# Linear attention with a highway layer: the softmax work of batches 2 and 3 and the key/value products moved in the order of issue

## The chip, the cores and the metric

One core of a Trainium2 chip runs the whole program. The metric is the device time of one execution in microseconds (us), the median of several. The kernel before takes 149.44 us (three runs, 148.86 to 149.5); the profiled execution has a span of 146.9 us from its first to its last instruction. The engines are TensorE (PE, with its weight loads PEld), VectorE (DVE), ScalarE (ACT), GpSimd (POOL) and SyncE, whose queue (SPq) issues every DMA. Each works through its own list of instructions in the order in which the program emits them.

## The reference

For each of 8 batches and 8 heads, q, k and v are 576 x 64. A softmax of q over the 64 features and one of k over the 576 positions stand on either side of a small product:

```
q_s = exp(q) / sum(exp(q), over features)
k_s = exp(k) / sum(exp(k), over positions)
kv  = k_s^T v          (64 x 64 per head)
x   = q_s kv           (heads side by side: 4608 rows of 512)
H = relu(x W_h);  T = sigmoid(x W_t + b_t);  out = T*H + (1-T)*x
```

The reference takes maxima off before the exponentials; the kernel does without. Its sigmoid is 0.5 + 0.5 tanh of half the argument.

## The kernel before

Each batch passes through two layers. The **attention part** of batch b consists of these helpers:

- `exp_half` (L150, two halves each for q and k, four heads a half): the exponentials, on ACT.
- `q_sums` (L195, two halves) and `q_recip` (L203), on DVE: the row sums of exp(q) and their reciprocals. Then the scaling of exp(q), for blocks 0 to 3 of its nine row blocks and for 4 to 8: `q_scale_p` (L214) does it on POOL, `q_scale_v` (L206) on DVE, with a small widening cast at L210 and a product at L212.
- `cast_v` (L160, two halves): v to 16 bits, on POOL unless another engine is given.
- `q_trans` (L218, groups of 4, 4 and 1 row blocks): transposes on PE, each followed by a copy from PSUM to `qsT` on DVE (L233).
- `kv_half` (L167, two halves of 36 small products into `psk`): needs half of exp(k) and the same half of the cast v. `kv_norm` (L183, DVE) then divides by the sums of exp(k) and gives `kvn`.
- `x_pair` (L235, two) and `x_left` (L259): the products of `qsT` and `kvn` on PE. Of the four copies of the pairs to `xT`, three are on ACT (L255) and the last on DVE (L257).

The **highway part** of batch c works in four column blocks `ob`: `gate` (four products of 512 columns, then a tanh on ACT, L288), `carry` (four products, then `dd` on DVE, L297) and `blend` (`g` on DVE, L305). `out_tile` turns a finished block back with transposes and copies it out on ACT (L336). The ninth row blocks of all batches (`x9`) form a last highway batch, c = 8.

The order of issue is written out by hand. The head, a list, holds batches 0 and 1 and the highway part of batch 0. From there on the program goes through numbered slots (`at`, L373): slot 8c + 2ob holds `gate(c, ob)`, slot 8c + 2ob + 1 holds `carry(c, ob)`, and slot 8c + 2ob + 2 holds `blend(c, ob)`. Thus eight slots, a stage, do the highway part of batch c and beside it the attention part of batch c + 1. For batch b the stage begins at slot p = 8(b - 1), and "step 3" of it is slot p + 3. Within a slot the functions come in the order in which they were registered, so gate or carry first, then blend, out_tile and the attention work. Whatever follows in the same engine's list waits behind an instruction that isn't ready.

PSUM is shared in rotation: four buffers (`ps_ht`) for gate and carry, so that a gate can start only when the blend two blocks earlier has read its buffer; three (`ps_q`, tag "qx") for `pq`, `psk` and `px`, eleven of which a batch uses in order; one for the output blocks (`nat`). Loads of q, k and v use three buffers each in SBUF, `ek` and `eq` two, `v16` two.

Of the kernel before, what the change touches and what calls it, by code (L numbers as in the profile page):

```python
# [18 lines left out]
def kernel(  # L19
# [10 lines left out]
    nc = tc.nc  # L30
    B, H, S, D = q.shape
    P = 128
    N9 = S // 64
# [339 lines left out]
    def at(p, *fs):  # L373
        events.setdefault(p, []).extend(fs)

    E = lambda f, *a: (lambda: f(*a))

    for c in range(1, B + 1):
        for ob in range(4):
            p = 8 * c + 2 * ob  # L380
# [6 lines left out]
    for g in range(B // 2):  # L387
        p = 16 * (g + 1)
# [5 lines left out]
                at(p + 1 + i // 2, E(out_tile, g, i, True))  # L394
    at(8 * B + 8, E(most9), E(last9))

    for b in range(2, B):
        p = 8 * (b - 1)
        s = p + {2: 0, 3: -4}.get(b, -5)
        at(s, E(exp_half, b, "q", 0))  # L400
        at(s + 1, E(exp_half, b, "q", 1), E(q_sums, b, 0))
        at(s + 2, E(q_sums, b, 1), E(q_recip, b), E(q_scale_p, b, 0, 4))
        if b == 2:
            at(s + 3, E(q_scale_v, b, 4, N9))
        else:
            at(s + 3, E(q_scale_p, b, 4, N9))
        s = p + {2: 2, 3: 0}.get(b, -1)
        at(s, E(exp_half, b, "k", 0))
        at(s + 1, E(exp_half, b, "k", 1))
        s += b == 2  # L410
        at(s, E(cast_v, b, 0))
        at(s + 1, E(cast_v, b, 1))
        tr, kv, x = {
            2: ((4, 4, 5), (5, 6), (7, 7, 7)),
            3: ((2, 3, 4), (4, 5), (6, 6, 7)),
        }.get(b, ((2, 3, 4), (2, 3), (4, 5, 6)))
        for i in range(3):
            at(p + tr[i], E(q_trans, b, i))
        at(p + kv[0], E(kv_half, b, 0))
        at(p + kv[1], E(kv_half, b, 1), E(kv_norm, b))  # L420
        at(p + x[0], E(x_pair, b, 0))
        at(p + x[1], E(x_pair, b, 1))
        at(p + x[2], E(x_left, b))
# [3 lines left out]
    for f in [  # L427
        E(warm_up, 20),
        E(exp_half, 0, "q", 0), E(q_sums, 0, 0),
        E(exp_half, 0, "q", 1), E(q_sums, 0, 1),  # L430
        E(q_recip, 0), E(q_scale_v, 0, 0, 4), E(q_scale_v, 0, 4, N9),
        E(exp_half, 0, "k", 0), E(cast_v, 0, 0),
        E(exp_half, 0, "k", 1), E(cast_v, 0, 1),
        E(q_trans, 0, 0), E(q_trans, 0, 1), E(warm_up, 2), E(q_trans, 0, 2),
        E(warm_up, 6),
        E(kv_half, 0, 0), E(gate_bias), E(warm_up, 2), E(kv_half, 0, 1), E(kv_norm, 0),
        E(warm_up, 4),
        E(x_pair, 0, 0), E(warm_up, 2), E(x_pair, 0, 1), E(warm_up, 2), E(x_left, 0),
        E(warm_up, 14),
        E(exp_half, 1, "q", 0), E(exp_half, 1, "q", 1),  # L440
        E(q_sums, 1, 0),
        *[E(cast_weight, "t", k_, nc.vector) for k_ in range(4)],
        E(q_sums, 1, 1), E(q_recip, 1), E(q_scale_v, 1, 0, 4), E(q_scale_v, 1, 4, N9),
        *[E(cast_weight, "h", k_, (nc.gpsimd, nc.scalar)[k_ % 2]) for k_ in range(4)],
        E(gate, 0, 0), E(gate, 0, 1), E(exp_half, 1, "k", 0), E(cast_v, 1, 0),
        E(carry, 0, 0), E(blend, 0, 0), E(carry, 0, 1), E(blend, 0, 1),
        E(exp_half, 1, "k", 1), E(cast_v, 1, 1),
        E(q_trans, 1, 0), E(q_trans, 1, 1), E(q_trans, 1, 2),
        E(gate, 0, 2), E(carry, 0, 2), E(blend, 0, 2),
        E(kv_half, 1, 0), E(gate, 0, 3), E(kv_half, 1, 1), E(kv_norm, 1),  # L450
        E(carry, 0, 3),
        E(x_pair, 1, 0), E(x_pair, 1, 1), E(blend, 0, 3), E(x_left, 1),
        *[E(load, b, w) for b in (2, 3) for w in "qkv"],
    ]:
        f()
    for p in range(8, 8 * (B + 1) + 1):
# [33 lines left out]
```

## Time and profile before

| engine | busy us (share of the span) |
|---|---|
| PE | 123.6 (84%) |
| DVE | 108.1 (74%) |
| ACT | 87.3 (59%) |
| POOL | 43.2 (29%) |

A stage can be timed by the start of the first product of `gate(c, 0)` in the trace of PE:

| stage (slots) | highway batch, attention batch | starts at us | length us |
|---|---|---|---|
| head | 0, and 0 and 1 | 0 | 34.17 |
| 8 to 15 | 1, 2 | 34.17 | 18.93 |
| 16 to 23 | 2, 3 | 53.10 | 12.39 |
| 24 to 31 | 3, 4 | 65.49 | 11.92 |
| 32 to 39 | 4, 5 | 77.41 | 13.82 |
| 40 to 47 | 5, 6 | 91.23 | 13.82 |
| 48 to 55 | 6, 7 | 105.05 | 13.82 |
| 56 to the end | 7, the ninth blocks, the last outputs | 118.87 | 28.03 |

The shares of the first table are means over stages that have different limits. How the lengths of the second come about is read from the timelines of the engines and from the chain of waits, which runs backwards from the last instruction to what released it.

### The profile page before, as it was taken

The page shows a single profiled execution, that of the slowest core. Times are in us where ns is not written, and L with a number is a line of the kernel's source. Part 1 is how long each engine was busy: PE and PEld are TensorE (multiplying, and loading weights), DVE is VectorE, ACT ScalarE, POOL GpSimd, SP SyncE. Part 2 cuts the span into 40 slices and gives each one's busy share as a digit, 9 for nine tenths or more (in the row PEclk, how much of TensorE's full clock was granted, in tenths as well). Part 3 has the DMA queues.
Part 4 walks back from the last instruction along what each step waited for, and adds up shares of the span by engine and source line. Part 5 has one row for each costly group of instructions (what it writes and reads, how often), then busy time and mean ns, then how long its engine had stood idle before and what let it go on. Part 6 is the DMA issues. An engine that isn't in the chain of part 4 may idle for free.

```text
span 146.9 us, 3530 instructions
## 1 busy us (share of the span) xinstructions
PE 123.6 (84%) x1477; PEld 67.9 (46%) x1477; DVE 108.1 (74%) x201; ACT 87.3 (59%) x126; POOL 43.2 (29%) x37
## 2 busy tenths in 40 slices
PE   4979999688528979979999599959977999999920
PEld 2335345233125336626645364634545455577610
DVE  1493589966997988996899399929983767577750
ACT  3660658336980269798499549936980764465420
POOL 2006011600083069059107900970295000000000
PEclk9999999999975899999999999999999999999996
DMA  4999999999999999403999999630051006047745
GB/s 159 357 402 397 401 400 410 412 414 403 411 408 412 407 411 412 161 0 145 271 407 416 322 411 402 279 149 0 4 228 60 4 0 286 0 176 326 288 178 179
DMA packets 16022, 40.06 MB, mean 273 GB/s; under 512 B 644, under 2 KB 1672, under 8 KB 14984
## 3 DMA queue, kind: packets, MB, share of 16 engines
q1 hardware_dynamic: 16008, 39.85, 70.6%
q8 instruction: 11, 0.18, 0.5%
q14 instruction: 3, 0.02, 0.0%
HBM read 30.41 MB, written 9.44 MB: 271 GB/s over the span
## 4 chain that ended last, share of the span: by engine, by line
PE 45%; DVE 29%; ACT 6%; POOL 6%; issue 4%; DMA 3%; POOLq 3%; SPq 0%; DVEq 0%; ACTq 0%
PE ph L59 14%; PE pt L59 12%; DVE r L199 10%; PE nat L59 6%; DVE dd L297 4%; PE psk L59 4%; POOL eq L216 3%; DVE eq L212 3%; DMA q<-in_q_dram 3%; DVE g L305 3%; POOLq L485 3%; PE pq L64 3%; PE warm L59 3%; PE px L59 3%; DVE qsT L233 2%
## 5 line engine op out<-in xcount | busy, mean ns | idle before, releaser
L288 ACT ACTIVATE pt<-pt,bt 128x512 f32<-128x512 f32 x36 | 24.0, 669 | 36.3 <-PE pt L59 35.9
L216 POOL TENSOR_TENSOR eq<-eq,r 128x1024 f16<-128x1024 f16 (+1 forms) x11 | 22.8, 2096 | 47.2 <-DVE r L204 34.7
L297 DVE SCALAR_TENSOR_TENSOR dd<-ph,xT 128x512 f16<-128x512 f32 x32 | 21.9, 683 | 17.0 <-PE ph L59 17.0
L59 PE MATMUL ph<-xT,w16h 128*128 128x512 f16 x128 | 33.7, 388 | 0.0
L59 PE MATMUL pt<-xT,w16t 128*128 128x512 f16 x128 | 33.2, 383 | 0.0
L305 DVE SCALAR_TENSOR_TENSOR g<-pt,dd 128x512 f16<-128x512 f32 x36 | 24.5, 680 | 1.9
L199 DVE TENSOR_REDUCE r<-eq 128x18 f32<-128x1152 f16 x16 | 21.6, 1347 | 4.4 <-ACT eq L154 4.2
L161 POOL CAST v<-v 128x1152 f16<-128x1152 f32 x16 | 18.6, 1184 | 13.3 <-DMA v<-in_v_dram 13.3
L154 ACT ACTIVATE eq<-q 128x1152 f16<-128x1152 f32 x16 | 18.5, 1173 | 2.6 <-DMA q<-in_q_dram 2.6
L154 ACT ACTIVATE ek<-k 128x1152 f16<-128x1152 f32 x16 | 18.7, 1185 | 2.0 <-DMA k<-in_k_dram 2.0
L59 PEld LDWEIGHTS <-w16t 128*128 128x128 f16 x144 | 12.8, 98 | 14.4 <-issue 1.4
L59 PE MATMUL nat<-half_i,g 128*128 128x128 f16 x140 | 18.7, 219 | 0.0
L59 PEld LDWEIGHTS <-w16h 128*128 128x128 f16 x144 | 12.4, 99 | 12.1 <-issue 1.7
L336 ACT COPY o<-nat 128x512 f32<-128x512 f32 x28 | 16.9, 603 | 1.7 <-issue 1.1
L255 ACT CAST xT<-px 128x512 f16<-128x512 f32 x24 | 13.4, 596 | 7.4 <-PE px L59 7.3
L64 PE MATMUL pq<-ident,eq 128*128 128x128 f16 x144 | 12.8, 231 | 5.7 <-POOL eq L216 4.1
L59 PE MATMUL nat<-ident,xT 128*128 128x128 f16 x128 | 17.3, 219 | 0.0
L59 PE MATMUL warm<-wide,ident 128*128 128x512 f16 x52 | 15.4, 446 | 1.9 <-DVE wide L140 1.9
L59 PEld LDWEIGHTS <-g 128*128 128x128 f16 x144 | 14.1, 98 | 3.8 <-DVE g L305 0.4
L64 PEld LDWEIGHTS <-eq 128*128 128x128 f16 x144 | 9.9, 103 | 9.5 <-POOL eq L216 4.6
L59 PEld LDWEIGHTS <-xT 128*128 128x128 f16 x128 | 12.5, 98 | 3.3
L59 PE MATMUL psk<-v,ek 64*64 64x65 f16 x576 | 8.1, 197 | 6.8 <-POOL v L161 5.5
(42 smaller groups left out, 91.6 us busy)
## 6 DMA issues: line engine op xcount, KB each, us to landing
out_dram<-o SPq DMA_DIRECT2D x8, 1024.0 KB, 4.3
q<-in_q_dram SPq DMA_DIRECT2D x7, 1152.0 KB, 13.6
k<-in_k_dram SPq DMA_DIRECT2D x7, 1152.0 KB, 14.6
v<-in_v_dram SPq DMA_DIRECT2D x6, 1152.0 KB, 14.6
v<-in_v_dram SPq DMA_DIRECT2D x4, 576.0 KB, 10.7
q<-in_q_dram SPq DMA_DIRECT2D x2, 576.0 KB, 4.0
k<-in_k_dram SPq DMA_DIRECT2D x2, 576.0 KB, 6.9
w32t<-in_moe_w_t_dram SPq DMA_DIRECT2D x1, 1024.0 KB, 12.9
```

Of the source, the lines that this page charges most:

```text
L59: mm = lambda o, l, r, st, sp: nc.tensor.matmul(o, l, r, start=st, stop=sp, skip_group_check=True)
L64: nc.tensor.matmul(o, i, ident, is_transpose=True, start=True, stop=True, skip_group_check=True,)
L154: nc.scalar.activation(dst[b][:, :, 2 * a : 2 * a + 2, :], in32[which][b][:, 2 * a : 2 * a + 2].rearrange("p c n d -> p n c d"), AF.Exp,)
L161: (eng or nc.gpsimd).tensor_copy(v16s[b % 2][:, :, 2 * a : 2 * a + 2, 0:64], in32["v"][b][:, 2 * a : 2 * a + 2].rearrange("p c n d -> p n ...
L199: nc.vector.reduce_sum(qsum[b][:, :, h], eq[b][:, :, h, :], axis=AX.X)
L212: nc.vector.tensor_mul(e, e, r2.unsqueeze(2).broadcast_to([P, w, 32, 2]))
L216: nc.gpsimd.tensor_mul(e, e, r.broadcast_to(list(e.shape)))
L255: nc.scalar.copy(dst, t[c])
L288: nc.scalar.activation(ps, ps, AF.Tanh, bias=bt2[:, ob : ob + 1], scale=0.5)
L297: nc.vector.scalar_tensor_tensor(dd, ps, 0.0, xv(ob), op0=ALU.max, op1=ALU.subtract)
L305: nc.vector.scalar_tensor_tensor(gv(ob), th, 1.0, dd, op0=ALU.add, op1=ALU.mult)
L336: nc.scalar.copy(o, flat(t))
```

## The change

It alters only the order of issue and which engine does two pieces of batch 2. Arithmetic, tiles and buffers stay.

- **Batch 2**: its exponentials of q go up into the head, between the products of batch 1, with the first half of the sums; the second half of the sums and the reciprocal stand first in slot 8. The second scaling is on POOL (`q_scale_p`) instead of DVE. The first half of v is cast on POOL ahead of the scaling, the second on DVE in slot 11. The key/value products come at steps 3 and 4, ahead of most transposes (4, 5, 5); the pairs come at steps 6 and 7.
- **Batch 3**: its exponentials of q move from slots 12 and 13 to 14 and 15, those of k stay in 16 and 17, both casts of v come before both scalings on POOL, and the transposes and products take the steps that batch 2 has.
- **Batch 4** gets what batch 3 had: exponentials of q at slots 20 and 21, of k at 24 and 25, products of k and v at steps 4 and 5, pairs at step 6.
- **Batches 5 to 7**: key/value products at steps 3 and 4 instead of 2 and 3, pairs and rest at 5, 6 and 7 instead of 4, 5 and 6.

The loads of batches 2 and 3 stand earlier in the text; the DMA queue holds the same order.

```diff
+    at(8, E(q_sums, 2, 1), E(q_recip, 2), E(cast_v, 2, 0), E(q_scale_p, 2, 0, 4))
+    at(9, E(exp_half, 2, "k", 0), E(q_scale_p, 2, 4, N9))
+    at(10, E(exp_half, 2, "k", 1))
+    at(11, E(cast_v, 2, 1, nc.vector))
     for b in range(2, B):
         p = 8 * (b - 1)
-        s = p + {2: 0, 3: -4}.get(b, -5)
-        at(s, E(exp_half, b, "q", 0))
-        at(s + 1, E(exp_half, b, "q", 1), E(q_sums, b, 0))
-        at(s + 2, E(q_sums, b, 1), E(q_recip, b), E(q_scale_p, b, 0, 4))
-        if b == 2:
-            at(s + 3, E(q_scale_v, b, 4, N9))
-        else:
-            at(s + 3, E(q_scale_p, b, 4, N9))
-        s = p + {2: 2, 3: 0}.get(b, -1)
-        at(s, E(exp_half, b, "k", 0))
-        at(s + 1, E(exp_half, b, "k", 1))
-        s += b == 2
-        at(s, E(cast_v, b, 0))
-        at(s + 1, E(cast_v, b, 1))
+        if b > 2:
+            s = p + {3: -2, 4: -4}.get(b, -5)
+            at(s, E(exp_half, b, "q", 0))
+            at(s + 1, E(exp_half, b, "q", 1), E(q_sums, b, 0))
+            at(s + 2, E(q_sums, b, 1), E(q_recip, b))
+            if b > 3:
+                at(s + 2, E(q_scale_p, b, 0, 4))
+                at(s + 3, E(q_scale_p, b, 4, N9))
+            s = p + {3: 0, 4: 0}.get(b, -1)
+            at(s, E(exp_half, b, "k", 0), E(cast_v, b, 0))
+            at(s + 1, E(exp_half, b, "k", 1), E(cast_v, b, 1))
+            if b == 3:
+                at(p + 1, E(q_scale_p, b, 0, 4), E(q_scale_p, b, 4, N9))
         tr, kv, x = {
-            2: ((4, 4, 5), (5, 6), (7, 7, 7)),
-            3: ((2, 3, 4), (4, 5), (6, 6, 7)),
-        }.get(b, ((2, 3, 4), (2, 3), (4, 5, 6)))
+            2: ((4, 5, 5), (3, 4), (6, 7, 7)),
+            3: ((4, 5, 5), (3, 4), (6, 7, 7)),
+            4: ((2, 3, 4), (4, 5), (6, 6, 7)),
+        }.get(b, ((2, 3, 4), (3, 4), (5, 6, 7)))
...
         E(kv_half, 1, 0), E(gate, 0, 3), E(kv_half, 1, 1), E(kv_norm, 1),
-        E(carry, 0, 3),
+        E(carry, 0, 3), *[E(load, b, w) for b in (2, 3) for w in "qkv"],
+        E(exp_half, 2, "q", 0),
         E(x_pair, 1, 0), E(x_pair, 1, 1), E(blend, 0, 3), E(x_left, 1),
-        *[E(load, b, w) for b in (2, 3) for w in "qkv"],
+        E(exp_half, 2, "q", 1), E(q_sums, 2, 0),
```

## The prediction

> **What bounds the kernel now.** I read the profile in this order: the stage lengths (starts of the first gate product), the PE timeline inside the long stages, then the chain of waits. PE has the most work, and a stage without a wait takes 11.92 us (24 to 31). Stages longer than that are paying for something.
>
> Stage 8 to 15 pays 7 us. The PE timeline shows what:
>
> ```profile
> 37.64 1.03 PE L59 MATMUL pt<-xT,w16t 128*128 128x512 f16 x4
> 42.78 1.04 PE L64 MATMUL pq<-ident,eq 128*128 128x128 f16 x8 [4.12 <-POOL eq L216]
> 44.55 1.03 PE L64 MATMUL pq<-ident,eq 128*128 128x128 f16 x8 [0.73 <-DVE eq L212]
> 45.37 1.91 PE L59 MATMUL ph<-xT,w16h 128*128 128x512 f16 x4
> ```
>
> The columns are start, time and instruction. PE runs out of gates and waits 4.12 us for the scaled exp(q) of batch 2, then 0.73 us more. The same carry products that take 0.87 us between neighbours elsewhere (36.77 to 37.64) then take 1.71 us (45.37 to 47.08): the view of busy time by stretch gives a granted clock of 0.50 from 42 to 48 us, 1.00 again from 49 us. The scaling is late because exponentials (35.83), sums and reciprocal (40.26) only begin with the stage, and because two engines collide:
>
> ```profile
> 40.82 1.90 POOL L216 TENSOR_TENSOR eq<-eq,r 128x1024 f16<-128x1024 f16 x1 [12.50 <-ACT ek L154]
> 42.67 2.83 POOL L161 CAST v<-v 128x1152 f16<-128x1152 f32 x2
> ```
>
> ```profile
> 41.10 1.66 DVE L210 CAST r<-r 128x40 f16<-128x40 f32 x1
> 42.80 1.69 DVE L212 TENSOR_TENSOR eq<-eq,r 128x1280 f16<-128x1280 f16 x1
> ```
>
> The small cast takes 1.66 us, ending as POOL's scaling ends; for batch 0 the chain has it at 0.11 us and the product at 0.83.
>
> Stages 32 to 55 pay 1.9 us each, always the same way (chain of waits; start, time, what):
>
> ```profile
> 77.46 0.39 DVE r L204
> ...
> 79.87 2.33 POOL eq L216
> 82.20 1.10 POOL v L161
> 83.34 0.48 PE psk L59 x36
> ...
> 89.96 1.29 DVE r L199
> ...
> 91.28 0.39 DVE r L204
> ```
>
> Reciprocal, two scalings and a cast on POOL lead to the key/value product, which stands at step 2 and waits 1.83 us (PE timeline); carry, dd and the next sums follow it, so the loop closes with 13.82 us.
>
> [...] half clock after a 4.1 us hole, full clock through holes of 1.83 us.
>
> **The change part by part.** All times from rows of the trace before; steps between neighbours on DVE are 0.61 (dd, g, copies), 1.26 to 1.39 (sums), 0.3 (reciprocal), a tanh can start 1.08 after its gate begins, likewise dd after carry.
>
> *Exponentials of q, batch 2.* q2's transfer was issued at 16.32 and landed 13.6 later, at 29.9. ACT idles 1.06 before 32.28 and 1.30 before 35.25; halves of 1.17 fit, at most 0.1 late. Cost nothing: hidden by these idle times. Sums and reciprocal follow x_left's copies on DVE (end 34.99): 1.26 + 1.39, reciprocal at 37.64 instead of 40.26. Queued behind them: dd(1,0), at 37.93 instead of 36.18, g(1,0) done 39.4, and gate(1,2) needs that PSUM buffer. It moves from 37.64 to 39.4; kv_half(2,0) (0.41) fills part, a hole of 1.35 us stays, too short for the clock.
>
> *Scaling and cast.* POOL starts 0.55 after the reciprocal's start (40.26 to 40.82, as before): 38.19 to 40.05; kv ahead of it needs only v2 (issued 21.07, landed 14.7 later, 35.8) and one cast. The removed DVE pair took 1.66 + 1.69 = 3.35; POOL's second scaling takes 2.33. New is the 128x1152 cast of v on DVE: the nearest row, DVE's 128x512 weight casts (four in 1.34, so 0.335 each), gives 0.75; [...]the sums (1.26 for the same size), is the upper end. I take 0.8. It is ready at 39.91 (g(1,0) 38.71 to 39.31, dd(1,1) to 39.91) while POOL scales, so it waits to 40.05 and ends 40.85; POOL's second scaling waits for it, 40.85 to 43.1. [...]
>
> *Rest of the stage.* kv_half(2,1) 40.9; carry(1,2) 41.35; second transposes 43.15, third to 43.9; gate(1,3) to 44.8; x_pair 44.9; ACT: tanh to 45.6, two px copies to 46.7. Here exp_half(3,q,0) now stands ahead of the third px copy: 1.05 to 47.75, copy to 48.3. gate(2,0) and x_left's last PSUM buffer wait for that copy, so the stage ends at about **48.5** instead of 53.10: 4.6 won. Without the clock loss it needs no other cause.
>
> *Stage 16 to 23* (12.39 now). Batch 3's second half of exp(q) ends near 49.4, after x_left and g(1,3) the sums end 52.0, so POOL starts near 52.5, two scalings end 54.4 and 56.7. The second transposes (step 5) wait for the latter; qsT copies, sums of batch 4 (1.26 + 1.39), g(2,2), reciprocal, dd and then DVE's xT copy follow, 63.1. gate(3,0)'s fourth product needs that copy. Counted as if it ran through, gate(3,0) starts at **62.4**, 13.9 later: 1.5 lost.
>
> *Stage 24 to 31* (11.92 now). POOL is no limit (its cast ends 67.6, kv_half at step 4 comes at 69.5). Both pairs stand at step 6: the fourth px buffer is the first's, so PE waits for tanh, out copy and px copy on ACT, 1 us in all. 13.0, gate(4,0) at **75.4**: 1.1 lost.
>
> *Stages 32 to 55.* kv_half at step 3 comes 5.4 after the stage's start. POOL's chain from the reciprocal: 0.55 + 4.2 + 1.1. The 1.83 wait goes. But x_pair(b,1) now comes after the next batch's sums and reciprocal on DVE. From kv_half's second half (7.4 after the start): kv_norm to 8.5, sums 9.76, dd 10.36, sums 11.75, reciprocal 12.04, g 12.6, xT copy 13.2. The next gate needs g's buffer (12.65) and in its fourth product the copy (13.25 - 0.65 for three products before it). So 12.65 instead of 13.82: POOL then has 0.5 to spare before kv_half. Two such stages win 1.17 each. In 48 to 55 no sums follow, DVE falls away and PE's own 12.05 is left: 1.77.
>
> *Sum*: -4.6 + 1.5 + 1.1 - 2 x 1.17 - 1.77 = -6.1; the 28.03 after slot 56 hold the same order. Cost nothing as well: the loads (batch 5 to 7 land over 10 us before use; the DMA share is 0.20 in 96 to 110).
>
> **The rivals.**
> *PE alone bounds*: waits of 1 us in the ACT and DVE lists don't arise, px copies slip in. Stage 8 to 15 12.5, then five of 12.0, 28.03 after: 34.17 + 12.5 + 60 + 28.03 = 134.7, so about 137 us. For it: DVE is busy only 10.98 of 13.80 us in 82.5 to 96.3. Against: the lists are in order, and their waits were counted above.
> *Half of it is given back*: [...] later pairs cost 13.2 a stage (+1.1): 146.7.
> *Slower*: the cast loses and a further hole brings the half clock back (+3.4 + 2.3 in stage 8 to 15), and xT behind the sums closes a loop of 13.8 as long as today's (+3.0 over three stages), with batch 3's late scaling costing another 1.0: 143.3 + 9.7 = 153. For it: the chain already runs through DVE in these stages. Against: holes in the new order stay below 2 us.
>
> **How the numbers follow.** As worked out, near 143.3: 0.55. PE alone or between, 137 to 140.5: 0.15. Half given back, 145 to 148.5: 0.20. Slower: 0.08, and 0.02 for nothing at all. The range 138.5 to 147 leaves out part of each outer case. Of "half given back" a little lies within 0.5%: faster 0.88, same 0.03, slower 0.09.
>
> **What will show it.** PE: no hole above 2 us in 34 to 49, clock 1.00 there; gate starts near 48.5, 62.4, 75.4, 88, 101, 113. POOL's cast row no longer releases psk from stage 32 on; gates are released by DVE g or xT instead. The DVE cast at L161 takes 0.8 to 1.3 us. ACT's third px copy of batch 2 starts after an exponential. Wrong if the half clock stays, if the cast takes over 2 us, or if stages 32 to 55 stay at 13.8.

## The result and the profile after

The changed kernel takes 141.33 us (median; 141.14 to 142.05) against 149.15 us before: the ratio is 0.948, 95% interval 0.944 to 0.953. The span of the profiled execution falls from 146.9 to 139.3 us. The forecast was 143.3 us. The medians here and below leave out executions in a slower state, 2 to 5 us longer, that most kernels show at times; of the traces only that of experiment 9 is of such an execution, and it lost its time in the head (38.64 us).

The stages, again by the first product of `gate(c, 0)`. Where that gate's fourth product waits, its start is counted as the fourth product's minus 0.65 us, as in the prediction (slot 24: 62.00 - 0.65; slot 32 on: 87.40 and 99.97 - 0.65):

| stage (slots) | before, us | forecast | after | after - before |
|---|---|---|---|---|
| head | 34.17 | 34.17 | 34.27 | +0.10 |
| 8 to 15 | 18.93 | 14.3 | 13.15 | -5.78 |
| 16 to 23 | 12.39 | 13.9 | 13.93 | +1.54 |
| 24 to 31 | 11.92 | 13.0 | 12.83 | +0.91 |
| 32 to 39 | 13.82 | 12.65 | 12.57 | -1.25 |
| 40 to 47 | 13.82 | 12.65 | 12.57 | -1.25 |
| 48 to 55 | 13.82 | 12.05 | 11.96 | -1.86 |
| 56 to the end | 28.03 | 28.03 | 28.02 | -0.01 |

The sum is -7.6 us, the difference of the spans. Between traces the head varies from 34.16 to 34.81 us, so its +0.10 says nothing; stages with the same order repeat closely (8 to 15 takes 13.14 or 13.15 us in experiments 1, 5, 6, 10 and 12 too).

The PE timeline of the changed kernel in stage 8 to 15 (start, time, instruction, idle time before it and what ended it):

```profile
38.71 1.02 PE L59 MATMUL pt<-xT,w16t 128*128 128x512 f16 x4 [0.40 <-DVE dd L297]
40.22 0.62 PE L64 MATMUL pq<-ident,eq 128*128 128x128 f16 x8 [0.49 <-POOL eq L216]
40.89 0.48 PE L59 MATMUL psk<-v,ek 64*64 64x65 f16 x36
41.30 1.04 PE L59 MATMUL ph<-xT,w16h 128*128 128x512 f16 x4
42.95 0.73 PE L64 MATMUL pq<-ident,eq 128*128 128x128 f16 x10 [0.61 <-POOL eq L216]
47.24 0.25 PE L59 MATMUL px_l<-qsT,kvn 64*64 64x64 f16 x4 [0.70 <-DVE xT L257]
```

The hole of 4.12 us is gone; the waits that are left are 0.4 to 0.7 us. The carry of four products keeps its 1.04 us where it took 1.91, at a granted clock of 1.00 instead of 0.50. The view of busy time by stretch shows it, one line of the kernel before and one of the changed kernel (stretch; length; busy time of PE, PEld, DVE, ACT and POOL; granted clock; share and GB/s of the DMA):

```profile
45.00:46.00 1.00, 1.00 (x8) 0.68 (x6) 1.00 (x3) 0.00 (x0) 0.50 (x1) 0.50 1.04 410
34.00:49.00 15.00, 12.59 (x150) 6.05 (x150) 13.54 (x27) 9.65 (x14) 8.02 (x5) 1.00 1.04 409
```

What PE waits for is the work of POOL and DVE, in the timelines of the changed kernel:

```profile
35.68 1.15 POOL L161 CAST v<-v 128x1152 f16<-128x1152 f32 x1 [7.56 <-DMA v<-in_v_dram]
38.26 4.64 POOL L216 TENSOR_TENSOR eq<-eq,r 128x1024 f16<-128x1024 f16 x2 [1.43 <-DVE r L204]
```

```profile
37.73 0.38 DVE L204 RECIPROCAL r<-r 128x36 f32<-128x36 f32 x1
39.96 0.88 DVE L161 CAST v<-v 128x1152 f16<-128x1152 f32 x1
```

POOL's scaling begins at 38.26 instead of 40.82. In every other pair of scalings it takes 4.19 us; here it takes 4.64, because DVE's cast gets in between the two: the cast ends at 40.84, 0.68 us after the first scaling (to 40.16), and the second, on record from 40.12, takes 2.78 us instead of 2.33.

In the later stages the chain of waits of the changed kernel no longer passes through POOL:

```profile
82.68 1.26 DVE r L199
83.94 0.60 DVE dd L297
84.54 1.27 DVE r L199
85.83 0.38 DVE r L204
86.21 0.55 DVE g L305
86.76 0.61 DVE xT L257
87.40 0.38 PE pt L59
```

The last line is one product, the fourth of `gate(5, 0)`. It waits for DVE's copy to `xT`, which stands behind the sums and the reciprocal of the next batch.

Two stages have grown. In 16 to 23 the fourth product of `gate(3, 0)` waits for DVE's copy, in 24 to 31 the second pair of batch 4 waits for a copy on ACT (PE timeline of the changed kernel):

```profile
62.00 0.38 PE L59 MATMUL pt<-xT,w16t 128*128 128x512 f16 x1 [0.84 <-DVE xT L257]
72.68 0.41 PE L59 MATMUL px<-qsT,kvn 64*64 64x512 f16 x3 [0.75 <-ACT xT L255]
```

### The profile page after: what moved, and what is told of

Its sections match the earlier page's. It is cut to its first block, busy times and chain, and to the rows that moved or that the text cites. A ratio compares the mean times of both kernels' runs of the same rounds, so it can differ in the third digit from the quotient of the medians.

```text
span 139.3 us, 3531 instructions
## 1 busy us (share of the span) xinstructions
PE 122.2 (88%) x1477; PEld 66.4 (48%) x1477; DVE 106.4 (76%) x200; ACT 88.1 (63%) x126; POOL 44.5 (32%) x37
## 4 chain that ended last, share of the span: by engine, by line
PE 50%; DVE 29%; ACT 5%; POOL 5%; DMA 3%; issue 3%; SPq 0%; DVEq 0%; POOLq 0%
PE pt L59 14%; PE ph L59 13%; DVE r L199 12%; PE nat L59 8%; POOL eq L216 5%; PE pq L64 4%; DVE g L305 4%; PE psk L59 3%; DMA q<-in_q_dram 3%; DVE dd L297 3%; PE warm L59 3%; ACT eq L154 2%; DVE eq L212 2%; PE px L59 2%; DVE r L204 2%
## 5 line engine op out<-in xcount | busy, mean ns | idle before, releaser
L216 POOL TENSOR_TENSOR eq<-eq,r 128x1024 f16<-128x1024 f16 (+1 forms) x12 | 25.6, 2153 | 30.2 <-DVE r L204 30.2
L59 PE MATMUL ph<-xT,w16h 128*128 128x512 f16 x128 | 32.8, 380 | 0.0
L161 POOL CAST v<-v 128x1152 f16<-128x1152 f32 x15 | 16.9, 1147 | 22.7 <-DMA v<-in_v_dram 20.9
L233 DVE COPY qsT<-pq 128x1024 f16<-128x1024 f16 (+1 forms) x24 | 12.8, 553 | 3.2 <-PE pq L64 3.0
L64 PE MATMUL pq<-ident,eq 128*128 128x128 f16 x144 | 11.5, 219 | 2.5 <-POOL eq L216 1.4
L64 PEld LDWEIGHTS <-eq 128*128 128x128 f16 x144 | 8.9, 98 | 6.4 <-POOL eq L216 3.1
## 6 DMA issues: line engine op xcount, KB each, us to landing
k<-in_k_dram SPq DMA_DIRECT2D x7, 1152.0 KB, 14.3
```

Source lines behind the costliest of these rows:

```text
L59: mm = lambda o, l, r, st, sp: nc.tensor.matmul(o, l, r, start=st, stop=sp, skip_group_check=True)
L64: nc.tensor.matmul(o, i, ident, is_transpose=True, start=True, stop=True, skip_group_check=True,)
L161: (eng or nc.gpsimd).tensor_copy(v16s[b % 2][:, :, 2 * a : 2 * a + 2, 0:64], in32["v"][b][:, 2 * a : 2 * a + 2].rearrange("p c n d -> p n ...
L216: nc.gpsimd.tensor_mul(e, e, r.broadcast_to(list(e.shape)))
L233: nc.vector.tensor_copy(qsT[b][:, :, n0:n1, :], t[:, :, 0:w, :])
```

## The experiments

Each kernel's ratio is to the kernel before, run beside it on the same chip; the changed kernel itself was not run again beside them. The intervals of the ratios are 0.3 to 1.3% wide, so differences of a few tenths of a us are read from the stages and not from the times.

**1. Batches 5 to 7 as before.**

```diff
-        }.get(b, ((2, 3, 4), (3, 4), (5, 6, 7)))
+        }.get(b, ((2, 3, 4), (2, 3), (4, 5, 6)))
```

> The changed kernel, but with batches 5 to 7 as they were before (key/value products at steps 2 and 3, pairs and rest at 4, 5, 6). Theory (the wait of the key/value product for POOL's cast is what the later steps remove): the wait comes back in at least two of the three stages from slot 32 on, which grow from about 12.5 to 13.8 us; 144.5 to 145.7 us in all. Rival (the later steps only trade that wait for one on DVE, and the gain of these stages came from batch 4's earlier start): within 1 us of the changed kernel's 141.3.

145.00 us, ratio 0.966 (0.960 to 0.973). The stages from slot 32 take 11.93, 15.37 and 13.82 us; two of them have the wait back. The theory holds, but 15.37 was not foreseen. The PE timeline of this kernel, then its busy time by stretch (columns as above):

```profile
92.12 0.48 PE L59 MATMUL psk<-v,ek 64*64 64x65 f16 x36 [1.84 <-POOL v L161]
95.36 1.57 PE L59 MATMUL pt<-xT,w16t 128*128 128x512 f16 x4
```

```profile
91.00:92.00 1.00, 0.00 (x0) 0.00 (x0) 0.01 (x1) 0.68 (x1) 1.00 (x1) 1.00 1.01 426
94.00:95.00 1.00, 1.00 (x28) 0.81 (x29) 0.84 (x2) 0.00 (x0) 0.00 (x0) 0.50 0.00 0
```

After a hole of only 1.84 us the clock stands at 0.50 for 3.42 us. The wait of 1.84 us and the half clock after it cost 3.4 us of stage (15.37 - 11.93) here; in the next stage the same wait, without the half clock, costs 1.9 (13.82 - 11.93).

**2. The same part alone, on the kernel before.**

```diff
-        }.get(b, ((2, 3, 4), (2, 3), (4, 5, 6)))
+            4: ((2, 3, 4), (2, 3), (4, 5, 6)),
+        }.get(b, ((2, 3, 4), (3, 4), (5, 6, 7)))
```

> The kernel before, with only batches 5 to 7 at the new steps (3 and 4; 5, 6, 7). Theory: the stages of 13.82 us become about 12.6, 12.6 and 12.0, with a rest of some 0.5 us of the wait in the first: 144.5 to 145.5 us, so a little over half of the whole gain. Rival (the two parts need each other, since POOL begins too late without the work on batches 2 to 4): 148 us or more.

145.48 us, ratio 0.974 (0.969 to 0.978). The three stages take 13.16, 12.57 and 11.96 us, with 0.47 us of the wait for POOL left in the first: together 3.8 us less than before. So the two parts don't need each other. The later steps bring 3.8 us alone. With both parts these three stages get 4.4 us shorter (the table); the rest of the gain, 3.2 us, comes from the head to slot 31, with batches 2 to 4.

**3. Both halves of v of batch 2 on POOL.**

```diff
-    at(8, ..., E(cast_v, 2, 0), E(q_scale_p, 2, 0, 4))
+    at(8, ..., E(cast_v, 2, 0), E(cast_v, 2, 1), E(q_scale_p, 2, 0, 4))
-    at(11, E(cast_v, 2, 1, nc.vector))
```

> The changed kernel, with both halves of v of batch 2 cast on POOL, in slot 8 ahead of the scaling; nothing on DVE. Theory (POOL is idle from 36.8 to 38.3 while it waits for the reciprocal, and the cast on DVE costs DVE 0.8 us [...]): the scaling begins as before and ends 0.45 us sooner, the stage is 0.3 to 0.5 us shorter, 140.8 to 141.0 us. Rival (two engines are needed, else the scaling starts late): 0.5 to 1.5 us slower than the changed kernel, 141.8 to 142.8.

141.20 us, ratio 0.9455 (0.942 to 0.949), between the two forecasts; the times alone can't tell it from the changed kernel. The POOL timeline of this kernel can:

```profile
35.99 2.24 POOL L161 CAST v<-v 128x1152 f16<-128x1152 f32 x2 [7.58 <-DMA v<-in_v_dram]
38.20 4.19 POOL L216 TENSOR_TENSOR eq<-eq,r 128x1024 f16<-128x1024 f16 x2
```

The scaling starts as early as with one cast and takes 4.19 us again; the stage takes 12.71 us instead of 13.15. Dividing the cast between two engines thus cost 0.44 us. It stood on DVE and held POOL up, while POOL had idle time for it.

**4. The kernel before, with the hole partly filled.** The products of `gate(1, 2)` are issued four times over.

```diff
+        for _ in range(4 if (c, ob) == (1, 2) else 1):
             for k_ in range(4):
                 mm(ps, w16["t"][:, k_, ob * P : ob * P + P], xv(k_), k_ == 0, k_ == 3)
```

> The kernel before, with the sixteen products of gate(1,2) issued four times over (each round overwrites the one before with the same values), so that PE works for 2.6 us of the hole of 4.1 us and nothing else changes. Theory (part of the loss in stage 8 to 15 is the half clock after the hole): granted clock 1.00 from 42 to 48 us, the stage 1.3 to 2.3 us shorter, 146.9 to 147.9 us. Rival (the engines behind PE set the pace there, so that the clock costs nothing): 148.8 to 149.5 us.

148.82 us, ratio 0.995 (0.992 to 0.998). PE timeline of this kernel:

```profile
37.85 3.62 PE L59 MATMUL pt<-xT,w16t 128*128 128x512 f16 x16
43.00 0.62 PE L64 MATMUL pq<-ident,eq 128*128 128x128 f16 x8 [1.53 <-POOL eq L216]
44.76 0.62 PE L64 MATMUL pq<-ident,eq 128*128 128x128 f16 x8 [1.15 <-DVE eq L212]
```

The clock stays at 1.00 throughout 38 to 49 us, and the stage takes 17.75 instead of 18.93 us. So the half clock cost 1.2 us of this stage, somewhat below the 1.3 to 2.3 expected: with it gone, PE waits longer for DVE. The median of the times, though, lies in the rival's range. The traced execution (148.01 us, granted clock 0.987 over its whole span) is one of the two fastest of nine; the other seven have 0.976 to 0.981 and spans 0.8 to 1.4 us longer. They seem to have lost the clock somewhere again; where, no trace shows. The 1.2 us rest on this one trace.

**5. The fourth px copy of batches 3 to 6 on ACT.**

```diff
-            if a + c < 2:
+            if a + c < (3 if 3 <= b <= 6 else 2):
```

> The changed kernel, with the fourth px copy of batches 3 to 6 on ACT too (it was on DVE behind the next batch's sums and reciprocal). Theory (that copy is what the first gate of a stage waits for, so it sets the 12.57 us of stages 32 to 47 and the 0.84 us hole at slot 24): the fourth product of gate(3,0), gate(5,0) and gate(6,0) no longer waits; stage 16 to 23 loses about 1 us, stages 32 to 47 come down to 12.0 to 12.2 us; 139.1 to 139.8 us in all. Rival (the loop through POOL is as long, or ACT becomes the bound with 0.5 us more a stage): within 0.5 us of 141.3, with a wait for POOL or ACT in the same place.

139.91 us, ratio 0.938 (0.933 to 0.942), just above the range of the theory. From slot 8 the stages take 13.15, 12.91, 12.94, 11.97, 12.20 and 12.20 us, against 13.15, 13.93, 12.83, 12.57, 12.57 and 11.96. No first gate waits any more, so DVE's copy was the bound of stages 16 to 23 and 32 to 47. The 12.20 is a new one, in the chain of waits of this kernel:

```profile
85.47 0.39 DVE r L204
...
87.88 2.33 POOL eq L216
90.21 1.10 POOL v L161
...
91.35 0.48 PE psk L59 x36
```

It is the loop through POOL, as in the kernel before, but with 12.20 us a round instead of 13.82. It takes some of the gain back, 0.24 us of it in stage 48 to 55.

**6. Batch 4 at the steps of batches 5 to 7.**

```diff
-            4: ((2, 3, 4), (4, 5), (6, 6, 7)),
```

> The changed kernel, with batch 4 at the steps of batches 5 to 7 (key/value products at 3 and 4, pairs and rest at 5, 6, 7 instead of 4, 5 and 6, 6, 7). Theory (stage 24 to 31 is long because both pairs stand together and PE waits 0.75 us for ACT's copy of the first): that wait goes, but gate(4,0) then waits for DVE's copy behind the sums as in the later stages, so the stage comes from 12.8 to 12.6 us; 141.0 to 141.3 us in all. Rival (POOL's cast of batch 4 is too late for step 3): a wait of psk for POOL, 141.5 us or more.

141.39 us, ratio 0.947 (0.943 to 0.951). PE's wait of 0.75 us for ACT's copy is gone, `gate(4, 0)` waits 0.43 us for DVE's copy instead, and the stage takes 12.57 us instead of 12.83. The trade was foreseen; in the time it doesn't show.

**7. The exponentials of q of batch 3 two slots earlier**, in ACT's idle time, the sums where they were.

```diff
-            at(s, E(exp_half, b, "q", 0))
-            at(s + 1, E(exp_half, b, "q", 1), E(q_sums, b, 0))
+            at(12 if b == 3 else s, E(exp_half, b, "q", 0))
+            at(13 if b == 3 else s + 1, E(exp_half, b, "q", 1))
+            at(s + 1, E(q_sums, b, 0))
```

> The changed kernel, with the two exponentials of q of batch 3 in slots 12 and 13, where ACT idles for 4.15 us, instead of 14 and 15; the sums stay. As the prediction had it (the exponential ahead of the third px copy holds gate(2,0) up by 1.05 us): gate(2,0) starts near 46.4, about 1 us less in all, 140.3 us. As the trace after has it (x_left waits for DVE's px copy, which ends at 47.18, and that hangs on POOL's scaling, not on ACT): gate(2,0) stays at 47.2 to 47.5, 141.1 to 141.4 us.

141.34 us, ratio 0.947 (0.943 to 0.951). `gate(2, 0)` starts at 47.16 us, the stage takes 12.79 us. So the exponential ahead of the copy cost 0.36 us of this stage and not 1.05; the next stage takes 14.05 instead of 13.93 us, which gives 0.12 back. PE timeline of this kernel:

```profile
46.98 0.25 PE L59 MATMUL px_l<-qsT,kvn 64*64 64x64 f16 x4 [0.35 <-ACT xT L255]
```

In the changed kernel the same product waited for DVE's copy until 47.24; here it starts while that copy still runs (46.60 to 47.28) and waits for ACT's third copy instead. So a copy on either engine can free its PSUM buffer, and the exponential cost only what the product loses by waiting for DVE's instead of ACT's.

**8. Three of these together** (3, 5 and 6).

```diff
-    at(8, ..., E(cast_v, 2, 0), E(q_scale_p, 2, 0, 4))
+    at(8, ..., E(cast_v, 2, 0), E(cast_v, 2, 1), E(q_scale_p, 2, 0, 4))
-    at(11, E(cast_v, 2, 1, nc.vector))
...
-            if a + c < 2:
+            if a + c < (3 if 3 <= b <= 6 else 2):
...
-            4: ((2, 3, 4), (4, 5), (6, 6, 7)),
```

> The changed kernel with three of these together: v of batch 2 cast on POOL alone, the fourth px copy of batches 3 to 6 on ACT, batch 4 at the steps of batches 5 to 7. Theory (each takes away a wait of its own): 0.4 + 1.0 + 0.8 + 1.1 us, 137.8 to 138.8 us. Rival (PE, DVE and the loop through POOL are so near each other that one gain uses the other's up): 139.5 us or more.

139.45 us, ratio 0.934 (0.931 to 0.938): outside the theory's range and 0.05 us short of the rival's. The stages from slot 8 take 12.69, 12.92, 12.61, 12.20, 12.20 and 12.20 us: the first two gains are whole, while from slot 24 on the loop through POOL leaves 0.7 us of the 1.9 that the theory counted. The PE timeline of this kernel shows it in two of its stages:

```profile
65.99 0.48 PE L59 MATMUL psk<-v,ek 64*64 64x65 f16 x36 [0.47 <-POOL v L161]
78.19 0.48 PE L59 MATMUL psk<-v,ek 64*64 64x65 f16 x36 [0.15 <-POOL v L161]
```

**9. The same, with the casts of v of batches 4 to 7 ahead of the scalings on POOL.**

```diff
-                at(s + 2, E(q_scale_p, b, 0, 4))
+                at(s + 2, E(cast_v, b, 0), E(cast_v, b, 1), E(q_scale_p, b, 0, 4))
...
-            at(s, E(exp_half, b, "k", 0), E(cast_v, b, 0))
-            at(s + 1, E(exp_half, b, "k", 1), E(cast_v, b, 1))
+            at(s, E(exp_half, b, "k", 0))
+            at(s + 1, E(exp_half, b, "k", 1))
+            if b == 3:
+                at(s, E(cast_v, b, 0), E(cast_v, b, 1))
```

> The combined kernel (v of batch 2 cast on POOL, fourth px copy of batches 3 to 6 on ACT, batch 4 at the common steps), and in addition the casts of v of batches 4 to 7 ahead of the scalings on POOL, in its idle time before the reciprocal. Theory (what is left in the combined kernel's stages of 12.20 us is the loop reciprocal, two scalings, cast, key/value product, sums, reciprocal): the waits of psk for POOL (0.47 and three of 0.15 us) go and the stages from slot 24 on come down to PE's own 11.95 to 12.05 us; 137.9 to 138.6 us in all. Rival (DVE or ACT is as near as POOL): stages of 12.15 us or more, 139.2 us or more.

138.34 us, ratio 0.927 (0.925 to 0.929): faster than both kernels. The stages from slot 24 on take 12.08, 11.98, 11.97 and 11.97 us, and no psk waits for POOL. Busy time by stretch in this kernel (columns as above):

```profile
84.00:96.00 12.00, 12.00 (x183) 6.93 (x171) 10.59 (x21) 10.69 (x17) 6.42 (x4) 1.00 0.91 362
```

PE has no hole, DVE and ACT have 1.3 us to spare in 12. From slot 32 on PE alone is the bound.

**10. The kernel of experiment 1 once more.**

> The kernel of the first experiment once more, for one look at its stage 40 to 47, which took 15.37 us there with half clock from 93.5 to 96.5 us after a hole of 1.84 us. Theory [...]: stage 40 to 47 at 13.8 or at 15.4 us, and if there is a half clock it may be in another stage. Rival (this order always loses the clock there): 15.4 us at the same place.

145.33 us in one run. Stage 40 to 47 takes 15.35 us, again after a hole of 1.83 us, with the clock at 0.50 from 92.90 to 96.32 us. Stage 48 to 55, with the same hole, takes 13.83 us and keeps the clock: the carry behind the hole takes 1.04 us there and 1.36 us in stage 40 to 47. The half clock came at the same place both times, which by itself doesn't tell chance from something in that order.

It lasts 3.42 us in both traces. In experiment 1 it begins at 93.06 us, 0.94 us after the end of the hole, and ends at 96.48, in the view of busy time by stretch (columns as above):

```profile
93.00:93.20 0.20, 0.20 (x2) 0.07 (x1) 0.00 (x0) 0.00 (x0) 0.16 (x1) 0.66 0.00 0
96.40:96.60 0.20, 0.20 (x2) 0.04 (x1) 0.20 (x1) 0.00 (x0) 0.00 (x0) 0.80 0.00 0
```

The length of the hole alone does not decide it: of two holes of 1.84 us in experiment 1, and of two of 1.83 us in experiment 10, one lost the clock and one kept it, and the three of the kernel before (1.83, 1.84 and 1.83 us) kept it (1.00 from 48.8 to 144.3 us). What tells them apart, these traces don't show. The times of experiment 1 speak against the rival's "always": two of its executions have a granted clock of 0.980 and 0.981, the third, not traced, 0.991 and a span 1.5 to 1.8 us shorter.

**11. The exponentials of q of batch 2 back in slots 8 and 9**, sums and reciprocal in 9 and 10, those of k in 10 and 11.

```diff
-    at(8, E(q_sums, 2, 1), E(q_recip, 2), E(cast_v, 2, 0), E(q_scale_p, 2, 0, 4))
-    at(9, E(exp_half, 2, "k", 0), E(q_scale_p, 2, 4, N9))
-    at(10, E(exp_half, 2, "k", 1))
+    at(8, E(exp_half, 2, "q", 0))
+    at(9, E(exp_half, 2, "q", 1), E(q_sums, 2, 0))
+    at(10, E(q_sums, 2, 1), E(q_recip, 2), E(cast_v, 2, 0), E(q_scale_p, 2, 0, 4))
+    at(10, E(exp_half, 2, "k", 0), E(q_scale_p, 2, 4, N9))
+    at(11, E(exp_half, 2, "k", 1))
```

> The changed kernel, with the exponentials of q of batch 2 and their sums back in slots 8 to 10 (those of k in 10 and 11), and all else of batch 2 as changed. Theory (the early start is what brings POOL's scaling from 40.8 to 38.3 us, and the second transposes hang on the scaling): the scaling starts at 40.6 to 41.0, stage 8 to 15 takes 15.4 to 15.8 instead of 13.15 us, 143.5 to 144.2 us in all. Rival (key/value products ahead of the transposes and the second scaling away from DVE are enough): below 142.3 us.

145.36 us, ratio 0.976 (0.973 to 0.979): 4.0 us slower than the changed kernel and more than expected. The scaling starts at 41.41 us, 6.6 us after the stage does, as in the kernel before; the stage takes 17.30 us. The clock is at 0.50 from 41.83 to 48.66 us, which the expectation had left out. It falls after a hole of 1.92 us, a wait for exp(k), which this edit makes late too, and as a second hole of 1.58 us begins (PE timeline of this kernel):

```profile
40.34 0.48 PE L59 MATMUL psk<-v,ek 64*64 64x65 f16 x36 [1.92 <-ACT ek L154]
43.37 1.04 PE L64 MATMUL pq<-ident,eq 128*128 128x128 f16 x8 [1.58 <-POOL eq L216]
```

DVE's cast meets POOL's first scaling at its beginning here, in the timelines of this kernel:

```profile
41.72 2.27 DVE L161 CAST v<-v 128x1152 f16<-128x1152 f32 x1
```

```profile
41.41 4.64 POOL L216 TENSOR_TENSOR eq<-eq,r 128x1024 f16<-128x1024 f16 x2 [4.17 <-ACT ek L154]
```

The cast that took 0.88 us takes 2.27.

**12. The casts of v ahead of the scalings, on the changed kernel alone.**

> The changed kernel, with nothing but the casts of v of batches 4 to 7 ahead of the scalings on POOL. Theory (in the changed kernel DVE's px copy behind the sums sets the stages of slots 32 to 47, POOL has time to spare): 141.0 to 141.6 us, gate(5,0) and gate(6,0) still waiting 0.43 us for that copy. Rival (POOL's loop is the bound there): 140.5 us or less.

141.31 us, ratio 0.948 (0.947 to 0.950): no change, and both gates still wait 0.43 us for DVE's copy. In the changed kernel POOL has time to spare; only with that copy out of the way (experiment 9 against 8) is its order worth anything.

## Why the prediction was right, and where it was off

- **Exponentials and reciprocal of batch 2, scaling on POOL.** Right: scaling from 38.26 (38.19 forecast); second scaling to 42.90 (43.1). Experiment 11 puts the early start of the exponentials, those of k with those of q, at 4.15 of the stage's 5.78 us, the half clock included.
- **The DVE cast.** Right: it ended at 40.84 (40.85 forecast), 0.68 us after the first scaling (40.16), and the second took 2.78 us instead of 2.33. Experiments 3 and 11 agree: without the cast the pair of scalings takes 4.19 instead of 4.64 us, and a cast that meets the first scaling 0.3 us after its start ends 0.7 us after its end (43.99 and 43.31, the latter from the 1.90 us that it takes in the changed kernel). What in the hardware holds the cast up, no trace shows.
- **"gate(1,2) needs that PSUM buffer. It moves from 37.64 to 39.4": wrong.** It started at 38.71, released by dd(1,0). The trace before had shown it: `gate(1, 2)` began at 37.64 us there, before the blend g(1,0) at 38.29, so it can't need the buffer which that blend reads. The account of the four buffers ahead of the prediction, which has a gate wait for the blend two blocks earlier, is wrong in the same way. This was off the path.
- **The end of stage 8 to 15 was the mis-sized term**: -4.6 forecast, -5.78 measured. Counted from the head's end, the pairs came 0.5 us earlier than reckoned (the scaling ended 0.2 us sooner, ten transposes took 0.57 instead of 0.75 us). Then "gate(2,0) and x_left's last PSUM buffer wait for that copy" on ACT was wrong: x_left waited for DVE's copy, which ended sooner, and gate(2,0) did not wait. From pairs to gate it took 2.94 instead of 3.6 us. Experiment 7 puts the exponential in front of the copy at 0.36 us instead of 1.05.
- **The half clock.** That it would go was right (1.2 us by the one trace of experiment 4). That holes of 1.83 us are safe, as the three of the kernel before were, does not hold in general: experiments 1, 10 and 11 lost the clock after holes of 1.83 to 1.92 us. The changed kernel, with no wait above 0.84 us from slot 8 to 55, never put it to the test.
- **Stages 16 to 23 and 24 to 31.** +1.5 and +1.1 forecast, +1.54 and +0.91 measured, by the waits named. Experiment 5 takes DVE's copy away and wins 1.02 us back in the first; experiment 6 takes the two pairs apart and wins 0.26 in the second.
- **Stages 32 to 55.** 12.65 forecast, 12.57 measured, and 12.05 against 11.96. Of the two releasers named, only the xT copy was real: with it on ACT (experiment 5) no gate waited for g.
- **The rivals.** PE alone as the bound came true only in experiment 9. The cast held up by both scalings (+2.3 us), and the loop of 13.8 us on DVE, did not come about.

The forecast missed 2.0 us of the time: 1.2 us of stage 8 to 15, some 0.4 of the later stages together, and 0.3 because it was counted from 149.44 us and not 149.15. The rest lies within the runs' own spread.

## What to carry to other kernels

When a wait is moved away, ask what stands next in the same list: here the loop went from POOL (13.82 us) to DVE's copy (12.57), back to POOL (12.20) and then to PE (11.97), and each step was worth what the next bound left of it. A copy that opens the next stage shouldn't stand behind reductions that nobody needs yet (experiment 5), and work whose inputs are there early (the cast of v) belongs ahead of work that waits, once that engine is the bound (experiment 9, not 12). Which buffer a product waits for is read from an earlier trace, by what started before what, rather than by counting buffers in rotation; a changed order can change it again (experiment 7).

## What the runs showed of the hardware

A hole of 1.84 us in PE's work was followed by half clock in one stage and not in the next with the same hole (experiment 1; experiment 10 likewise with 1.83 us). The half clock lasted 3.42 us in experiments 1 (93.06 to 96.48 us) and 10 (92.90 to 96.32 us), where PE was busy throughout it, and 6.83 us in the kernel before (41.96 to 48.79 us) and in experiment 11 (41.83 to 48.66 us), where PE stood idle for 1.5 us of it.

A DVE cast of 128x1152 from 32 to 16 bits took 0.88 us when it began 0.2 us before the end of a scaling on POOL (changed kernel), and 2.27 us when it began 0.3 us after the start of one (experiment 11).
